# RWKV5 time mixing into a top-1 mixture of experts: order by half sequences, two padded loads a unit, w2 loads spread over the units, gate product as column tiles

## The chip, the cores and the metric

One core of a Trainium2 chip runs the whole program. Its engines work side by side and wait for each other through semaphores: TensorE (PE, with its weight loads PEld), VectorE (DVE), ScalarE (ACT), GpSimd (POOL) and SyncE (SP). Here SP issues most loads and stores; ACT issues the w2 loads and POOL the gathers and scatters by index. The metric is the device time of one execution in microseconds (us); the lower, the better.

## The reference

Two blocks follow each other. The first is a linear recurrence with 4 batches, 8 heads, 768 tokens and head size 48; the second sends each of the 3072 tokens to one of 8 experts.

```python
for t in range(S):                       # attention block, per batch and head
    cur = einsum('bhd,bhe->bhde', u * k[t], v[t])
    y[t] = einsum('bhd,bhde->bhe', r[t], state + cur)
    state = w * state + einsum('bhd,bhe->bhde', k[t], v[t])
x = y.transpose(0, 2, 1, 3).reshape(B * S, H * D)      # 3072 x 384
logits = x @ w_gate                      # 8 experts
expert = argmax(logits); gate = softmax(logits)[expert]
for e in range(8):                       # each token through its expert
    out[expert == e] = gate * (relu(x[expert == e] @ w1[e]) @ w2[e])
```

All tensors are float32.

## The kernel before, in words

**Two halves.** `fast()` computes the time mixing, `experts()` the routing and the experts. A branch on the decay values (`wi`, L78) picks `fast()` or a slower general form; with these inputs it is `fast()`. All engines read `wi` before they branch.

**Time mixing in chunks.** The sequence is cut into 6 chunks of 128 tokens. Two heads form a pair (`hp`, 4 of them), and a unit is three chunks of a pair: 4 batches x 4 pairs x 2 halves are 32 units. Unit `2i` and unit `2i + 1` are the two halves of pair `i`.

- `u_load` (L409) loads a pair on SP's queue with six DMAs: rT and kT (48 partitions for each head), kt (tokens on partitions) and V.
- `u_scale` (L420) multiplies by decay tables: K (L429), RK (L433) and Kg (L435) on POOL, R (L431) on DVE.
- `u_scores` (L439): twelve records of score products P (L448) on PE, then the u term in one column (L454). ACT copies that column (`dv`, L458) and writes six scaled identities A (L462); DVE copies P over them under a mask (L464).
- `u_state` (L472): state products Gp (L479) and the running states St on DVE (L484, L486).
- `u_out` (L489): yp from states (L501) and from A (L505), two column tiles of 64, copied by ACT to y (L508).
- `u_gate` (L510): for one chunk of 128 tokens of a batch, four products of y with IW (identity blocks and gate weights, 104 columns) into rp. ACT copies x to xb (L516), DVE reduces the logits to lg (L517). After the sixth chunk `choose` (L105) makes softmax and choice on DVE and ACT and writes xb to HBM (L125).

**Order.** Inside `manual_schedule` (L531) each engine runs its instructions in the order of the code. A step `u` issues, in this order, a pair's loads (even u), `u_scale(u + 2)`, `u_scores(u + 1)`, `u_state(u + 1)`, `u_out(u)` and one gate product, if a finished batch has some left. Six gate products of the last batch remain behind the loop.

**Tables and other loads.** The decay chain (L379 to L400) starts inside `fast()`, after the branch: seven levels of powers on DVE, two reciprocals, four transposes on PE (w3p). POOL first clears the tiles whose unused partitions must be zero (L348). All eight w2 slices (1.5 MB each) are issued on ACT's queue ahead of the branch (L725).

**DMA lanes.** Every DMA of SP and ACT takes one of eight semaphore lanes (DMAHW0 to DMAHW7) in turn, and its issue waits until the DMA that had the lane before has landed.

**Experts.** 28 tiles of 128 tokens: a gather of xs by index (L664), a load of w1 (L662), three transposes, 24 products to the hidden layer, eight to the result, a scatter.

## Time and profile before

| | us |
|---|---|
| median of 3 runs | 541.81 (541.66 to 541.88) |
| profiled execution | 540.06 |
| its span | 538.3 |
| TensorE busy | 449.0 (83%) |
| ScalarE, VectorE, GpSimd busy | 125.5, 146.6, 158.3 |

The profile is of one execution. A busy share says little here, because the program has stages with different limits: at its start loads and tables are made, then the units of time mixing run, then the last gate products and the routing, then the experts. So a view by stage comes first, then in each stage who waits for whom, and in the stage in which TensorE is busy, the chain that ended last.

In a row of the timeline or of the groups, `out<-in` names the tiles, `x12` is the number of records merged, and what stands in brackets is the engine's idle time before it and what ended that. A float32 matmul leaves two records. SPq and ACTq are the DMA issues of those queues.

### The profile page before, as it was taken

Reading aid. Unit: us, or ns where it says so; the run is one execution under the profiler, and the core shown is the slowest. Engines: PE = TensorE matmul, PEld = TensorE weight load, DVE = VectorE, ACT = ScalarE, POOL = GpSimd, SP = SyncE. Lnnn points to the kernel's source line nnn. Section 1 sums busy time; section 2 is a strip of 40 time slices with the busy share of each in tenths; the row PEclk is TensorE's granted clock in tenths of the full one; section 3 lists DMA queues with packets and bytes.
Section 4 is the critical chain, followed back from the end, with each engine's and each line's share of the span. In section 5 each row is a group of like instructions: output and inputs, shape, how many; then the busy total and the mean of one; then the engine's idle time right before and its main releaser. Section 6 shows DMA issues by size and latency. Waiting matters only on the chain.

```text
span 538.3 us, 9970 instructions
## 1 busy us (share of the span) xinstructions
PE 449.0 (83%) x3893; PEld 377.4 (70%) x3893; DVE 146.6 (27%) x376; ACT 125.5 (23%) x373; POOL 158.3 (29%) x181
## 2 busy tenths in 40 slices
PE   0027889899899730399999999999999999999994
PEld 0016889799889620288778877887788778877882
DVE  5212875646646318001010101011110101010100
ACT  0023767556557310011001100110001100110010
POOL 6017977557384000211112111211121112211220
PEclk9999999969889855599999999999999999999999
DMA  7998665385480223634554465445544554455450
GB/s 252 367 380 211 172 177 149 113 195 166 133 221 5 89 88 141 254 136 167 207 195 158 161 209 199 161 162 185 214 159 154 183 224 151 163 172 224 161 172 16
DMA packets 21900, 94.80 MB, mean 176 GB/s; under 512 B 4128, under 2 KB 7238, under 8 KB 16980
## 3 DMA queue, kind: packets, MB, share of 16 engines
q1 hardware_dynamic: 16980, 70.83, 40.5%
q0 software_dynamic: 3712, 10.64, 6.4%
q10 hardware_dynamic: 1152, 12.58, 6.3%
q8 instruction: 35, 0.57, 0.5%
q14 instruction: 21, 0.17, 0.1%
HBM read 84.59 MB, written 10.24 MB: 176 GB/s over the span
## 4 chain that ended last, share of the span: by engine, by line
PE 70%; DMA 10%; issue 9%; DVE 6%; ACT 3%; POOL 1%; ACTq 1%; POOLq 0%; DVEq 0%; SPq 0%
PE hp L685 25%; PE yp L693 23%; DMA w_all<-in_moe_w_dram 7%; PE rp L514 5%; PE P L448 4%; PE yp L505 4%; PE P L454 3%; PE yp L501 3%; PE Gp L479 2%; ACT A L462 2%; PE xTp L672 2%; DMA xs<-x_hbm,idx 1%; DVE St L486 1%; DMA x_hbm<-xb 1%; DVE A L464 1%
## 5 line engine op out<-in xcount | busy, mean ns | idle before, releaser
L685 PEld LDWEIGHTS hp<-xT,w1s 128*128 128x128 f32 x1344 | 155.8, 194 | 8.2 <-DVE xT L674 1.1
L685 PE MATMUL hp<-xT,w1s 128*128 128x128 f32 x1344 | 156.1, 277 | 0.6 <-DVE xT L674 0.6
L693 PE MATMUL yp<-w_all,hT 128*128 x448 | 149.1, 486 | 0.0
L693 PEld LDWEIGHTS yp<-w_all,hT 128*128 128x128 f32 x448 | 83.0, 190 | 51.8
L687 ACT ACTIVATE hT<-hp 128x512 f32<-128x512 f32 x56 | 33.4, 597 | 296.8 <-PE hp L685 296.8
L697 POOL DMA_INDIRECT out_dram<-yo,idx x28 | 28.5, 1019 | 248.9 <-DVE yo L696 248.9
L462 ACT ACTIVATE A<-ident,dv 128x128 f32<-128x128 f32 x192 | 59.6, 389 | 0.1
L674 DVE COPY xT<-xTp 128x384 f32<-128x384 f32 x29 | 16.2, 558 | 152.9 <-PE xTp L672 152.9
L429 POOL TENSOR_TENSOR K<-kT,W 128x384 f32<-128x384 f32 x32 | 36.2, 1132 | 57.3 <-DMA kT<-in_k_dram 31.7
L696 DVE TENSOR_SCALAR yo<-yp,xs 128x384 f32<-128x384 f32 x28 | 17.3, 618 | 129.0 <-PE yp L693 129.0
L448 PE MATMUL P<-R,K 48*128 48x128 f32 x384 | 32.7, 307 | 19.2 <-POOL K L429 15.2
L464 DVE COPY_PREDICATED A<-mask,P 128x384 f32<-128x384 int32 x64 | 33.9, 583 | 50.0 <-ACT A L462 42.7
L664 POOL DMA_INDIRECT xs<-x_hbm,idx x30 | 29.4, 981 | 56.0 <-DVE idx L650 47.2
L448 PEld LDWEIGHTS P<-R,K 48*128 48x128 f32 x384 | 26.3, 204 | 24.1 <-POOL K L429 15.7
L505 PE MATMUL yp<-A,V 128*64 128x128 f32 x384 | 42.1, 297 | 1.2 <-DVE A L464 1.1
L501 PE MATMUL yp<-R,St 128*64 128x128 f32 x320 | 35.0, 299 | 0.0
L433 POOL TENSOR_TENSOR RK<-rT,kT 128x384 f32<-128x384 f32 x32 | 34.5, 1078 | 0.0
L514 PE MATMUL rp<-IW,y 128*128 128x104 f32 x192 | 31.1, 312 | 4.0 <-DVE lg L517 4.0
L514 PEld LDWEIGHTS rp<-IW,y 128*128 128x128 f32 x192 | 26.7, 215 | 8.6 <-DVE lg L517 5.1
L505 PEld LDWEIGHTS yp<-A,V 128*64 128x64 f32 x384 | 26.9, 152 | 1.6 <-DVE A L464 1.6
L431 DVE TENSOR_TENSOR R<-rT,W 128x384 f32<-128x384 f32 x32 | 23.5, 737 | 14.6 <-DMA rT<-in_r_dram 10.3
L454 PEld LDWEIGHTS P<-wu,RK 48*128 48x128 f32 x384 | 26.8, 206 | 0.2 <-POOL RK L433 0.2
(109 smaller groups left out, 241.8 us busy)
## 6 DMA issues: line engine op xcount, KB each, us to landing
w1s<-in_moe_w_dram SPq DMA_DIRECT2D x30, 1536.0 KB, 6.8
w_all<-in_moe_w_dram ACTq DMA_DIRECT2D x8, 1536.0 KB, 20.1
x_hbm<-xb SPq DMA_DIRECT2D x4, 1155.0 KB, 5.6
rT<-in_r_dram SPq DMA_DIRECT2D x32, 144.0 KB, 3.8
kT<-in_k_dram SPq DMA_DIRECT2D x32, 144.0 KB, 3.8
kt<-in_k_tokens_dram SPq DMA_DIRECT2D x16, 288.0 KB, 4.5
V<-in_v_dram SPq DMA_DIRECT2D x16, 288.0 KB, 4.0
xs<-x_hbm,idx POOLq DMA_INDIRECT x30, 3.1
```

Source lines behind the costliest of these rows:

```text
L429: nc.gpsimd.tensor_tensor(x["K"], m["kT"][:, tt].rearrange("p (c t) -> p c t", t=C), bc(W2[:, hp, None, :], [128, HC, C]), op=ALU.mult)
L433: nc.gpsimd.tensor_tensor(x["RK"], m["rT"][:, tt], m["kT"][:, tt], op=ALU.mult)
L448: nc.tensor.matmul(P[hi][:, c * C:(c + 1) * C], lhsT=x["K"][q, c, :], rhs=x["R"][q, c, :], start=True, stop=True, skip_group_check=True)
L454: nc.tensor.matmul(P[hi][:, o:o + 1], lhsT=x["RK"][q, c * C:(c + 1) * C], rhs=wu[q, 1, hp:hp + 1], start=True, stop=True, skip_group_check ...
L462: nc.scalar.activation(A[:, hi, c, :], ident, func=ACT.Copy, scale=dv[:, hi, c:c + 1])
L464: nc.vector.copy_predicated(A[:, hi], bc(mask[:, None, :].bitcast(I32), [128, HC, C]), P[hi][:, 0:HC * C].rearrange("p (c t) -> p c t", c=HC))
L501: nc.tensor.matmul(yp[q, c, :], lhsT=m["St"][:, g, hi, :], rhs=x["R"][:, c, :], start=True, stop=False, skip_group_check=True)
L505: nc.tensor.matmul(yp[q, c, :], lhsT=vh(x, c, hi, 64), rhs=x["A"][:, hi, c, :], start=g == 0, stop=True, skip_group_check=True)
L514: nc.tensor.matmul(rp[:, hp, :], lhsT=pairs[b * HP + hp]["y"][:, ch * C:(ch + 1) * C], rhs=IW[:, hp, :], start=True, stop=True, skip_group ...
L685: nc.tensor.matmul(p[:, f, :], lhsT=m["w1"][:, d, o:o + 128], rhs=m["xT"][:, d, :], start=d == 0, stop=d == DT - 1)
L687: nc.scalar.activation(m["hT"][:, 4 * fb:4 * fb + 4, :], p, func=ACT.Relu)
L693: nc.tensor.matmul(p, lhsT=m["hT"][:, f, :], rhs=w2_all[:, ds(m["e"], 1), f * DM:(f + 1) * DM], start=f == 0, stop=f == FT - 1)
```

## The change

- **Order.** Units go by half sequences: for each batch the first halves of the four pairs, then the second halves. A unit takes its incoming state from the unit four back.
- **Loads.** The host packs r and k of a unit into one array, padded with zeros to 128 partitions, and v and k by tokens into another. A unit is two DMAs of 384 and 288 KB; before, half a pair was two of 144 KB and one of 288 KB. Rings of four and five buffers for them, and the buffers for R, K, RK and Kg, lie in the space of w2's last three slices. The first four units are issued ahead of the branch; `u_load(u + 4)` is issued at step u.
- **w2.** Slices 0 to 4 are issued on ACT's queue at steps 1, 5, 9, 13 and 17, slices 5 to 7 behind the loop.
- **Tables.** w and u come as one load on ACT's queue; the powers are made ahead of the branch. The tables for pair 0 are made first, two copies go to ACT, and one reciprocal is left. No tiles are cleared on POOL but IW and a mask.
- **Scores.** The u products stand ahead of the score products, RK ahead of K, one dv copy instead of two. There are three A tiles instead of four.
- **Gate.** A gate product is eight column tiles of 64 tokens. A half's three chunks are multiplied in the first three steps of the next half, so three are left behind the loop; these use the buffers of rp and yp. There is one xb tile instead of two.

On SP's queue, ahead of and behind the branch: `rT`, `kT`, `kt`, `V` are a pair's loads, IW the gate weights; in brackets what an issue waits for. Before:

```order
L727 TENSOR_LOAD wi [waits DVE_49]
L729 COMPARE_AND_BRANCH
L414 DMA rT_135<-in_r_dram 48x768 [waits DMAHW7_49,Pool_49]
L415 DMA kT_131<-in_k_dram 48x768 [waits DMAHW0_49]
L414 DMA rT_135<-in_r_dram 48x768 [waits DMAHW1_49]
L415 DMA kT_131<-in_k_dram 48x768 [waits DMAHW2_49]
L365 DMA IW<-in_moe_w_gate_heads_dram 48x4x8 [waits DMAHW3_49,Pool_49]
L365 DMA IW<-in_moe_w_gate_heads_dram 48x4x8 [waits DMAHW4_49]
L417 DMA kt<-in_k_tokens_dram 128x576 [waits DMAHW5_49]
L418 DMA V_147<-in_v_dram 128x576 [waits DMAHW6_49]
L414 DMA rT_136<-in_r_dram 48x768 [waits DMAHW7_49]
```

Now (`in_r_k_units` and `in_v_k_units` are a unit's two loads, written to the ring in w2's tile):

```order
L85 DMA w_all<-in_v_k_units_dram 128x576
L84 DMA w_all<-in_r_k_units_dram 128x768 [waits DMAHW0_49]
L85 DMA w_all<-in_v_k_units_dram 128x576 [waits DMAHW1_49]
L84 DMA w_all<-in_r_k_units_dram 128x768 [waits DMAHW2_49]
L85 DMA w_all<-in_v_k_units_dram 128x576 [waits DMAHW3_49]
L739 TENSOR_LOAD wi [waits DVE_49]
L741 COMPARE_AND_BRANCH
L512 DMA IW<-in_moe_w_gate_heads_dram 48x4x8 [waits DMAHW4_49,Pool_49]
L512 DMA IW<-in_moe_w_gate_heads_dram 48x4x8 [waits DMAHW5_49]
L84 DMA w_all<-in_r_k_units_dram 128x768 [waits DMAHW6_49,DVE_49]
L85 DMA w_all<-in_v_k_units_dram 128x576 [waits DMAHW7_49]
```

Four units' loads stand ahead of TENSOR_LOAD and the branch, where there was none, and the load of unit 4 stands behind IW.

On PE's queue, from the end of one unit's products to the next unit's, with a gate product between: `yp` is the unit's output, `rp` the gate product, `P` the scores. Before:

```order
L501 MATMUL yp<-R,St 64x128 x2
L505 MATMUL yp<-A_141,V_149 64x128 x2
L514 MATMUL rp<-IW,y 128x104 x4
L448 MATMUL P_943<-R,K 128x128
L448 MATMUL P_944<-R,K 128x128
```

Now (the ring's tiles read `w_all`):

```order
L495 MATMUL yp<-w_all,St 64x128 x2
L499 MATMUL yp<-A_157,w_all 64x128 x2
L527 MATMUL rp<-IW,y 64x104 x8
L447 MATMUL P<-wu,w_all 128x1 x6
L452 MATMUL P<-w_all 128x128 x6
L475 MATMUL Gp<-w_all 48x48 x6
L495 MATMUL yp<-w_all,St 64x128 x2
```

The gate product went from four products of 128 columns to eight of 64, and the u products (128x1) went ahead of the scores.

On ACT's queue, the end of the time mixing: `y` and `xb` are its copies of the unit's output and of the gate product, `ex` the choice's exponential, `hT` the experts' first step. Before, from the last unit on:

```order
L458 COPY dv<-P_2186 128x3
L458 COPY dv<-P_2187 128x3
L462 ACTIVATE A_142<-ident,dv 128x128 x6
L508 COPY y<-yp 128x384 x2
L516 COPY xb<-rp 128x384 x6
L112 ACTIVATE ex<-sub 128x48
L687 ACTIVATE hT<-hp 128x512 x56
```

Now, behind the loop:

```order
L502 COPY y<-yp 128x384
L529 COPY xb<-rp 128x384
L502 COPY y<-yp 128x384
L563 DMA w_all<-in_moe_w_dram 128x3072 x3
L529 COPY xb<-rp 128x384 x3
L150 ACTIVATE ex<-sub 128x48
L701 ACTIVATE hT<-hp 128x512 x56
```

Six gate copies behind the last unit became three, and three w2 loads stand between the last unit's copy and them.

The core of the diff:

```diff
+    wu = consts.tile([128, 2, HP], FP32, name="wu")
+    nc.scalar.dma_start(wu, wu_in)
+
+
+    ring = w2_all[:, E - 3:, :].rearrange("p e f -> p (e f)")
+    at = [0]
+
+    def cut(n, size):
+        ts = [ring[:, at[0] + i * size:at[0] + (i + 1) * size] for i in range(n)]
+        at[0] += n * size
+        return ts
+
+    rks = cut(4, 2 * HC * C)
+    toks = cut(5, 4 * HC * D)
+    Rs, Ks, RKs, Kgs = cut(3, HC * C), cut(2, HC * C), cut(2, HC * C), cut(2, 2 * HC * D)
+
+    def unit(u):
+
+        return u // (2 * HP), u // HP % 2, u % HP
+
+    def u_load(u):
+        b, hf, hp = unit(u)
+        nc.sync.dma_start(rks[u % 4], rk[b, hf, hp])
+        nc.sync.dma_start(toks[u % 5], tok[b, hf, hp])
+
+    for i in range(4):
+        u_load(i)
...
+    Wp = consts.tile([128, HP, C], FP32, name="Wp")
+    Wr = consts.tile([128, HP, C], FP32, name="Wr")
+    pw = consts.tile([128, LV + 1, HP], FP32, name="pw")
+    nc.gpsimd.memset(Wp[:, :, 0:1], 1.0)
+    nc.gpsimd.memset(Wr[:, :, C - 1:C], 1.0)
+    nc.vector.tensor_copy(pw[:, 0, :], wu[:, 0, :])
+    for l in range(LV):
+        n = 1 << l
+        wn = bc(pw[:, l, :, None], [128, HP, n])
+        nc.vector.tensor_tensor(Wp[:, :, n:2 * n], Wp[:, :, 0:n], wn, op=ALU.mult)
+        nc.vector.tensor_tensor(Wr[:, :, C - 2 * n:C - n], Wr[:, :, C - n:C], wn, op=ALU.mult)
+        nc.vector.tensor_tensor(pw[:, l + 1, :], pw[:, l, :], pw[:, l, :], op=ALU.mult)
+    wC = pw[:, LV, :]
...
+        As = [ca.tile([128, 2, HC, C], FP32, name=f"A{i}") for i in range(3)]
+
+        Gp = ps.tile([128, HC, 2, 64], FP32, name="Gp", tag="g", bufs=1)
+        nc.vector.memset(Gp, 0.0)
...
+        inv = ca.tile([128, HP, 64], FP32, name="inv")
+
+        def tables(h0, h1):
+            hs = slice(h0, h1)
+            n = h1 - h0
+            nc.vector.reciprocal(inv[:, hs], Wp[:, hs, 1:65])
+            nc.scalar.copy(W2[:, hs, 0:64], Wr[:, hs, 64:])
+            nc.scalar.copy(W2[:, hs, 64:], inv[:, hs])
+            nc.vector.tensor_tensor(W1[:, hs, 0:64], Wp[:, hs, 0:64], bc(inv[:, hs, 63:64], [128, n, 64]),
+                                    op=ALU.mult)
+            nc.scalar.copy(W1[:, hs, 64:], Wp[:, hs, 0:64])
+
+        def tables_g(h0, h1):
+            hs = slice(h0, h1)
+            n = h1 - h0
+            W3 = As[2].rearrange("p h c t -> p (h c t)")[:, 0:HP * C].rearrange("p (a t) -> p a t", a=HP)
+            nc.vector.tensor_tensor(W3[:, hs], Wr[:, hs], bc(pw[:, LV - 1, hs, None], [128, n, C]), op=ALU.mult)
+            w3p = ps.tile([128, HP, C], FP32, name="w3p", tag="rw", bufs=1)
+            for hp in range(h0, h1):
+                nc.tensor.transpose(w3p[:, hp, :], W3[:, hp, :], ident)
+            nc.scalar.copy(Wg[:, hs], w3p[:, hs].rearrange("p a (h d) -> p a h d", h=2)[:, :, :, 0:D])
...
-            nc.gpsimd.tensor_tensor(x["K"], m["kT"][:, tt].rearrange("p (c t) -> p c t", t=C),
-                                    bc(W2[:, hp, None, :], [128, HC, C]), op=ALU.mult)
-            nc.vector.tensor_tensor(x["R"], m["rT"][:, tt].rearrange("p (c t) -> p c t", t=C),
-                                    bc(W1[:, hp, None, :], [128, HC, C]), op=ALU.mult)
-            nc.gpsimd.tensor_tensor(x["RK"], m["rT"][:, tt], m["kT"][:, tt], op=ALU.mult)
+            nc.gpsimd.tensor_tensor(x["RK"], x["r"], x["k"], op=ALU.mult)
+            nc.gpsimd.tensor_tensor(x["K"], x["k"], bc(W2[:, hp, None, :], [128, HC, C]), op=ALU.mult)
+            nc.vector.tensor_tensor(x["R"], x["r"], bc(W1[:, hp, None, :], [128, HC, C]), op=ALU.mult)
...
-            P = x["P"] = [ps.tile([128, 512], FP32, name=f"P{hi}", tag=f"P{hi}", bufs=2) for hi in range(2)]
-            for c in range(HC):
-                for hi in range(2):
-                    q = slice(64 * hi, 64 * hi + D)
-                    nc.tensor.matmul(P[hi][:, c * C:(c + 1) * C], lhsT=x["K"][q, c, :], rhs=x["R"][q, c, :],
-                                     start=True, stop=True, skip_group_check=True)
+            hp, A = x["hp"], x["A"]
+            P = ps.tile([128, 2, 512], FP32, name="P", tag="P", bufs=2)
             for c in range(HC):
                 for hi in range(2):
                     q = slice(64 * hi, 64 * hi + D)
                     o = HC * C + c
-                    nc.tensor.matmul(P[hi][:, o:o + 1], lhsT=x["RK"][q, c * C:(c + 1) * C],
+                    nc.tensor.matmul(P[:, hi, o:o + 1], lhsT=x["RK"][q, c, :],
                                      rhs=wu[q, 1, hp:hp + 1], start=True, stop=True, skip_group_check=True)
+            for c in range(HC):
+                for hi in range(2):
+                    q = slice(64 * hi, 64 * hi + D)
+                    nc.tensor.matmul(P[:, hi, c * C:(c + 1) * C], lhsT=x["K"][q, c, :], rhs=x["R"][q, c, :],
+                                     start=True, stop=True, skip_group_check=True)
             dv = ap2.tile([128, 2, HC], FP32, name="dv")
-            for hi in range(2):
-                nc.scalar.copy(dv[:, hi, :], P[hi][:, HC * C:HC * C + HC])
-            A = x["A"] = As[u % NA]
+            nc.scalar.copy(dv, P[:, :, HC * C:HC * C + HC])
...
+            x["y"] = ca.tile([128, HC * C], FP32, name="y", tag="y", bufs=8)
+            nc.scalar.copy(x["y"], yp.rearrange("p c t -> p (c t)"))
...
+                gx[b] = (ca.tile([128, G, W], FP32, name="xb"), sm.tile([128, G, E], FP32, name="lg"))
+            xb, lg = gx[b]
+            ch = hf * HC + c
+            rp = ps.tile([128, HP, 2 * D + E], FP32, name="rp", tag=tag, bufs=bufs)
             for hp in range(HP):
-                nc.tensor.matmul(rp[:, hp, :], lhsT=pairs[b * HP + hp]["y"][:, ch * C:(ch + 1) * C],
-                                 rhs=IW[:, hp, :], start=True, stop=True, skip_group_check=True)
+                y = units[h * HP + hp]["y"]
+                for j in range(2):
+                    q = slice(64 * j, 64 * j + 64)
+                    nc.tensor.matmul(rp[q, hp, :], lhsT=y[:, c * C + 64 * j:c * C + 64 * j + 64],
+                                     rhs=IW[:, hp, :], start=True, stop=True, skip_group_check=True)
...
-
-        gates = []
+            if ch == G - 1:
+                choose(b, xb, lg)
+
         gx = {}
 
-        def gate_step():
-            b, ch = gates.pop(0)
-            if ch == 0:
-                gx[b] = (ap2.tile([128, G, W], FP32, name="xb"), sm.tile([128, G, E], FP32, name="lg"))
-            u_gate(b, ch, *gx[b])
-            if ch == G - 1:
-                choose(b, *gx[b])
-
         with tc.manual_schedule():
-            u_load(0)
-            u_load(1)
+            tables(0, 1)
             u_scale(0)
+            tables_g(0, HP)
+            u_scale_g(0)
+            tables(1, HP)
+            u_scores(0)
             u_scale(1)
-            u_scores(0)
+            u_scale_g(1)
+            gate_weights()
             u_state(0)
             for u in range(NU):
-                if u % 2 == 0 and u // 2 + 2 < B * HP:
-                    u_load(u // 2 + 2)
+                if u + 4 < NU:
+                    u_load(u + 4)
+                if u % 4 == 1 and u // 4 < E - 3:
+                    nc.scalar.dma_start(w2_all[:, u // 4, :], w2[u // 4])
                 if u + 2 < NU:
                     u_scale(u + 2)
+                    u_scale_g(u + 2)
                 if u + 1 < NU:
                     u_scores(u + 1)
                     u_state(u + 1)
                 u_out(u)
-                if gates:
-                    gate_step()
-                if u % (2 * HP) == 2 * HP - 1:
-                    gates += [(u // (2 * HP), ch) for ch in range(G)]
-            while gates:
-                gate_step()
+                if u >= HP and u % HP < HC:
+                    u_gate(u // HP - 1, u % HP, "rw", 1)
+            for e in range(E - 3, E):
+                nc.scalar.dma_start(w2_all[:, e, :], w2[e])
+            u_gate(NU // HP - 1, 0, "rw", 1)
+            u_gate(NU // HP - 1, 1, "y", 2)
+            u_gate(NU // HP - 1, 2, "y", 2)
...
-    for e in range(E):
-        nc.scalar.dma_start(w2_all[:, e, :], w2[e])
```

## Rows read from the trace of the kernel before

**Rows 1.** Stages: start:end, length; busy PE, PEld, DVE, ACT, POOL; clock, DMA share, GB/s.

```profile
0.00:44.64 44.64, 4.46 (x40) 3.95 (x40) 13.19 (x45) 3.37 (x9) 13.90 (x33) 1.00 0.89 317
44.64:180.20 135.56, 126.14 (x1903) 116.77 (x1901) 84.41 (x214) 85.15 (x300) 86.47 (x91) 0.94 0.59 155
180.20:201.65 21.45, 10.70 (x51) 8.97 (x50) 2.62 (x15) 3.59 (x8) 0.00 (x0) 0.59 0.19 69
...
224.00:538.30 314.30, 306.32 (x1879) 246.32 (x1879) 33.49 (x57) 33.43 (x56) 54.91 (x55) 0.99 0.48 168
```

**Rows 2.** Waits of SP's queue, 0 to 45 us: total, times, longest.

```profile
SPq L415 <- DMA w_all<-in_moe_w_dram: 11.4, 2, 6.6
...
SPq L365 <- DMA w_all<-in_moe_w_dram: 8.0, 2, 4.4
```

**Rows 3.** Timeline, first 53 us: start, length, engine, line, tiles; idle before and releaser.

```profile
2.94 0.54 DVE L73 TENSOR_REDUCE wx<-wrow 1x1 f32<-1x384 f32 x1 [1.57 <-DMA wrow<-in_w_row_dram]
...
7.97 0.54 DVE L379 COPY pw<-wu 128x4 f32<-128x4 f32 x1 [2.64 <-DMA wu<-in_w_dram]
...
14.42 1.69 DVE L392 RECIPROCAL W<-Wp 128x256 f32<-128x256 f32 x1
...
16.80 1.09 PE L398 MATMUL w3p<-ident,W 128*128 128x128 f32 x4 [16.80 <-DVE W L395]
...
31.40 0.99 POOL L429 TENSOR_TENSOR K<-kT,W 128x384 f32<-128x384 f32 x1 [18.78 <-DMA kT<-in_k_dram]
...
44.64 1.65 PE L448 MATMUL P<-R,K 48*128 48x128 f32 x12
...
47.30 0.56 PE L479 MATMUL Gp<-V,Kg 128*48 128x48 f32 x8
```

**Rows 4.** DMA listing, all: queue, count, KB each, median us to landing.

```profile
x_hbm<-xb SPq DMA_DIRECT2D x4, 1155.0 KB, 5.6
...
wu<-in_w_dram SPq DMA_DIRECT2D x2, 0.8 KB, 6.0
```

**Rows 5.** Line L726 (the w2 loads on ACT's queue): ns of an issue, min/median/max.

```profile
L726 ACTq DMA_DIRECT2D w_all<-in_moe_w_dram x8: 334/448/797, 0.8 to 10.6; - x8
```

**Rows 6.** Timeline of PE: first score matmuls of four time-mixing steps.

```profile
57.44 0.94 PE L448 MATMUL P<-R,K 48*128 48x128 f32 x12
...
64.34 0.94 PE L448 MATMUL P<-R,K 48*128 48x128 f32 x12
...
79.22 0.94 PE L448 MATMUL P<-R,K 48*128 48x128 f32 x12
...
95.53 0.94 PE L448 MATMUL P<-R,K 48*128 48x128 f32 x12
```

**Rows 7.** Chain that ended last, 83 to 88 us: one step with a gate product.

```profile
83.52 0.87 PE P L448 x12
84.39 0.56 PE P L454 x11
84.95 0.32 PE Gp L479 x8
...
85.50 0.22 PE yp L501 x4
...
86.37 1.07 PE rp L514 x8
```

**Rows 8.** Timeline: two waits after a routing choice.

```profile
104.90 0.96 PE L448 MATMUL P<-R,K 48*128 48x128 f32 x12 [2.22 <-DVE R L431]
...
150.32 1.02 POOL L429 TENSOR_TENSOR K<-kT,W 128x384 f32<-128x384 f32 x1 [9.44 <-DMA kT<-in_k_dram]
```

**Rows 9.** Timeline of the tail: gate product, last routing choice, first routing step.

```profile
184.00 1.89 PE L514 MATMUL rp<-IW,y 128*128 128x104 f32 x8 [0.80 <-DVE lg L517]
...
195.15 0.20 DVE L108 TENSOR_REDUCE mx<-lg 128x6 f32<-128x48 f32 x1
...
201.65 0.36 DVE L573 COPY rk<-rkp 128x192 f32<-128x192 f32 x1 [4.55 <-DMA x_hbm<-xb]
```

201 lines of the change are left out of this document (77 added, 124 removed).

## The prediction

> **What bounds the kernel now.** I first read busy time by stage [rows 1]. There are four stages: 44.64 us before the second score product, 135.56 us of time mixing, 21.45 us of tail, and, after 22.35 us of routing and first gather, 314.30 us of experts. TensorE is busy for 306 of the last stage's 314 us, and the change does not touch that code. It is busy for 4.46 us of the first stage and 10.70 us of the tail, so these two hold most of the idle time.
>
> Second, who waits in the first stage. The four loads of a pair stand on SP's queue. Of its time, 11.4 us before the kT issues and 8.0 us before the IW issues go to w2 transfers [rows 2]: a load's issue waits for a semaphore lane (DMAHW) that a w2 load took before it, so the loads go out one by one as the w2 slices land. GpSimd has its first K at 31.40 us, after 18.78 us of idle time that ends with the kT load; the steady loop begins at 44.64 us [rows 3].
>
> Third, the loop. A step without a gate takes 3.45 us, (64.34 - 57.44) / 2; one with a gate takes 4.08 us, (95.53 - 79.22) / 4 [rows 6]. In the gated step the chain is TensorE alone: 0.87 + 0.56 + 0.32 + five products at 0.22 + 1.07 = 3.92 us [rows 7]; with six products and a state product of 3 chunks it is 4.2. Without the gate that leaves 3.0 us, so the ungated step waits some 0.45 us for others. All 32 steps at these rates: 9.0 for the first two (44.64 to 53.63, slow clock), 18 x 4.08, 11 x 3.45 and 1.4 for the last step, 121.8 us. The loop took 135.6. The 13.8 us of difference lie at the three routing choices inside it: VectorE's choice delays R, and TensorE waits 2.22 us; the xb write stands on SP's queue ahead of the next loads, and a K waits 9.44 us for kT [rows 8]; the clock then falls (0.94 over the stage [rows 1]).
>
> Fourth, the tail. Six gate products stand one behind another, since each needs the one rp buffer back: 1.89 us of product after 0.80 us of waiting [rows 9]. The first routing step waits 4.55 us for the xb write.
>
> **Start: -28.2 us.** Loads of four units are issued before the branch and no w2 load is ahead of them, so the decay chain is next. Before, it runs from 7.97 (pw) to 17.89 (the end of w3p), 9.9 us [rows 3]. To this are added two reductions at 0.54, and the branch, which I put at 0.6; the two full reciprocals (1.7 each) shrink to a quarter of one, 0.4, ahead of W3, and two copies go to ACT: about 8.9 us. It starts when wu has landed. That is at about 3.0 us if it lands like wrow (2.94 [rows 3]), 3.5 us later if it takes the 6.0 us of the old wu loads [rows 4]. So w3p ends near 12. Unit 0's scores take 2.66 us (44.64 to 47.30) and its state product 0.6, and P of unit 1 starts near 15.5 by TensorE. GpSimd's queue holds RK, K, Kg of unit 0 and RK, K of unit 1 in a row at 1 us each, which allows 15 to 16.5. I take 16.4 for the point that was 44.64. The bounds are 14.5 and 20: -30 to -24.6. The first steps at slow clock are kept as they are.
>
> **Loop: -6.6 us.** Three gate products come into it (21 instead of 18).
> The gate product becomes eight column tiles of 64. The nearest row is u_out's pair of column tiles at 0.22 us for 128 columns [rows 7]; with 104 columns, four pairs cost 0.72 to 0.88, and 1.07 is the upper bound. I take 0.85, so a gated step is 3.85.
> As to the Trainium skill, TensorEngine Tiling (Array Packing), section Restrictions and Gotchas: column tiling and the fast weight load exclude each other. By that rule, with nothing gained, a gate would stay at 1.07 and the loop be 4.6 us longer; the 0.22 us pair, which loads its 64-column weights within that time, speaks for the smaller value.
> RK's product moves ahead of the scores, so ACT's A chain starts 0.87 us sooner; one dv copy is saved. An ungated step falls from 3.45 towards TensorE's 3.0: 3.2. Then 9.0 + 21 x 3.85 + 8 x 3.2 + 1.4 = 116.9 us. The order by half sequences leaves the number of state instructions as it is.
> The choices remain on VectorE's queue ahead of the next R, and the RK product now in front of P covers 0.6 of the 2.22 us. A load is issued four units ahead, so the 9.44 us wait should go. But two things are added. The x tile has one buffer, not two: the first gate copy of a batch waits on ACT for the xb write of the batch before (5.6 us to landing [rows 4]), and behind it stand dv and six A copies, for which VectorE and then TensorE wait. And five w2 loads now run beside the units' loads, at 0.45 us of ACT each to issue [rows 5], which ACT's idle time (85 busy of 136 us [rows 1]) hides. I take 4 us for each of three choices, 12 in all: 129 us against 135.6. The bounds are 0 and the old 13.8 with no gain at gates or ungated steps (+6.8) and 3 us for xb: 117 to 141.
> The loads themselves: a unit moves 0.69 MB, padding included; 22.0 MB of units, 7.9 of w2 and 3.5 of xb make 33.4 MB in the loop. The old loop moved 155 GB/s at a DMA share of 0.59, so 263 GB/s would fill the engines [rows 1]: 127 us of transfers. That is close to the loop's length, and closer still while w2 runs (rival 2).
>
> **Tail: -14.7 us.** Three gates remain, on three buffers (rw and the two of y). Products 2.6 us, beside them ACT: y copy 0.5, three w2 issues at 0.45 [rows 5], three xb copies at 0.5, then the last reduction 0.2, about 3.9 us after the last u_out; choice and two rank products took 1.95 (195.15 to 201.65 - 4.55 [rows 9]). The wait of 4.55 us for xb goes, because the routing tile no longer waits for a DMA. Some 6.8 us with handovers, against 21.45: bounds 5.5 and 9.5. In its place comes nothing on VectorE; the xb write is next, and only the gather needs it, some 15 us later.
>
> **Routing and experts: 0.** The same instructions; the last three w2 slices land during routing. Bounds -1 and +3.
>
> **Sum.** 540.06 us of the profiled execution (span 538.3) - 28.2 - 6.6 - 14.7 = 490.6. The median of the runs is 1.75 us above that execution, so I give **492.3 us**. By the bounds of the terms, 476 to 514.
>
> **Rivals.**
> 1. The choices stay as dear as they are, or the xb copy's wait on ACT replaces the late load and the clock falls again: loop 141, 504 us. For it: a stall of 2 us was enough before [rows 8]. Against: four units of loads ahead.
> 2. The transfers bound the first half. Eighteen steps, 69 us, have 12.4 MB of units, 7.9 of w2 and 1.2 of xb: 21.5 MB, 82 us at 263 GB/s, so +13 less the 4 that a choice would have cost anyway: 501 us. Against: the start moved 317 GB/s [rows 1], at which 21.5 MB take 68 us.
> The Trainium skill, Trainium Kernel Development and Optimization, section Key Constraints, says that transfers from the SP, ACT and POOL queues share the same 16 DMA engines and interleave; by it w2 on ACT's queue takes its time from the units' loads, as rival 2 has it.
> 3. Everything hides: no stall at a choice, loop 117, 480 us. Against: VectorE's choice is as long as before.
> 4. The last w2 slices hold up the xb write and with it the gather. They are 4.7 MB, 15 us at 317 GB/s, with xb's 5.6 behind them: 21 us, about when the gather asks. If it is late, +6: 498 us.
> 5. The start does not do what it says: the branch, ACT's copies and GpSimd's queue put 44.64 at 25, not 16.4: 501 us.
> 6. Slower than before. If the small padded rows beside w2 and xb moved no faster than the old loop's mean of 155 GB/s, 33.4 MB would need 215 us against 129: 578 us. It decides below 33.4 MB / 178 us = 188 GB/s. Against: 0.59 is the share at 155, the engines were not full.
>
> **How the numbers follow.** Forecast 0.56, rivals 1 to 6: 0.13, 0.09, 0.11, 0.04, 0.05, 0.02. The forecast's own spread is about 485 to 499; the range takes in rivals 2, 4, 5 and part of 1 and 3: 481 to 503 us. Only rival 6 is slower: slower by over 0.2% (about what a measurement of this kernel can tell from no change) 0.02, within 0.2% 0.01, faster 0.97.
>
> **What would show it.** Start: the second unit's first score product near 16 us and SP's queue without waits for w_all. Loop: gated steps near 3.85 us, rp groups near 0.85; at each choice look for ACT's xb copy waiting for x_hbm<-xb and for K waiting for a unit's load. Tail: some 7 us from the last yp to rk, whose wait is for PE, not a DMA. Wrong would be: a DMA share near 1 through the first half, K waiting for loads in most steps, or a gather later than the index by more than 8 us.

## The result and the profile after

Median of the runs 493.63 us (492.04 to 494.36), before 541.73 us; the ratio is 0.911 with an interval of 0.909 to 0.914. The forecast was 492.3 us. The profiled execution took 493.97 us with a span of 492.2 us, against 540.06 and 538.3 us before: 46.1 us less, where the terms summed to 49.5. The median hides part of that gap, because the profiled execution of before was 1.67 us under its median and this one is 0.3 us above its own. So the 1.3 us by which the median missed is not the size of the errors; those stand in the stages.

The stages of the kernel after, cut at the points that answer to [rows 1] (second score product, first gate product of the tail, first routing copy, first expert product; columns: start:end, length, busy time of PE, PEld, DVE, ACT and POOL, granted clock, DMA share, GB/s):

```profile
0.00:19.14 19.14, 5.97 (x52) 5.30 (x53) 11.70 (x39) 5.18 (x15) 11.05 (x30) 1.00 0.42 145
19.14:147.66 128.52, 119.18 (x2081) 109.75 (x2082) 86.00 (x217) 84.76 (x272) 84.07 (x89) 0.97 0.69 241
147.66:153.43 5.77, 2.87 (x54) 2.24 (x50) 2.05 (x11) 2.01 (x5) 0.00 (x0) 1.00 0.75 268
153.43:178.22 24.79, 2.30 (x28) 1.85 (x28) 13.37 (x46) 0.00 (x0) 3.08 (x3) 0.51 0.91 351
178.22:492.20 313.98, 306.95 (x1876) 247.25 (x1876) 32.93 (x56) 33.44 (x56) 55.00 (x55) 0.98 0.49 172
```

| stage | before, us | after, us | moved | forecast |
|---|---|---|---|---|
| start, to the second score product | 44.64 | 19.14 | -25.5 | -28.2 |
| loop, to the first product of the tail | 135.56 | 128.52 | -7.0 | -6.6 |
| tail, to the first routing copy (rk) | 21.45 | 5.77 | -15.7 | -14.7 |
| routing and first gather, to the first expert product | 23.92 | 24.79 | +0.9 | 0 |
| experts | 312.73 | 313.98 | +1.25 | 0 |

(The first expert product of before begins 1.55 us behind the 224.02 at which the stage of [rows 1] was cut, at 225.57 us, so the last two lines are cut there.)

**Start.** The timeline of the kernel after (start, length, engine, line, tiles; in brackets the idle time before and what ended it):

```profile
2.56 0.17 DVE L107 COPY pw<-wu 128x4 f32<-128x4 f32 x1 [2.56 <-DMA wu<-in_w_u_dram]
...
13.50 1.63 PE L452 MATMUL P<-w_all 48*128 48x128 f32 x12
...
17.09 1.05 DVE L460 COPY_PREDICATED A<-mask,P 128x384 f32<-128x384 int32 x2 [4.40 <-ACT A L458]
...
18.03 0.96 DVE L428 TENSOR_TENSOR w_all<-w_all,W 128x384 f32<-128x384 f32 x1
...
19.14 1.66 PE L452 MATMUL P<-w_all 48*128 48x128 f32 x12 [1.99 <-DVE w_all L428]
```

Against [rows 3] the decay chain starts at 2.56 instead of 7.97 us, and w3p ends at 12.27 (forecast: near 12). The waits of SP's queue for w2 in [rows 2] have no successor: no wait of that queue before 45 us names a w2 load. What is new is the last wait: the second score product stands for 1.99 us until VectorE has made R of unit 1, and VectorE had been standing in front of unit 0's predicated copies, which wait for ScalarE's A tiles.

**A choice.** In the same view, step 11, where before there was [rows 8]:

```profile
65.06 0.85 DVE L157 SCALAR_TENSOR_TENSOR eq<-sub,rev_e 128x48 f32<-128x48 f32 x1
...
67.18 0.94 PE L452 MATMUL P<-w_all 48*128 48x128 f32 x12 [1.57 <-DVE w_all L428]
...
67.89 0.72 DVE L482 SCALAR_TENSOR_TENSOR St<-St,pw,Gp 128x128 f32<-128x128 f32 x2
...
68.71 0.56 PE L475 MATMUL Gp<-w_all 128*48 128x48 f32 x8 [0.59 <-issue]
...
70.34 0.67 PE L499 MATMUL yp<-A,w_all 128*64 128x128 f32 x4
...
...
72.67 0.48 ACT L529 COPY xb<-rp 128x384 f32<-128x384 f32 x1 [0.29 <-PE rp L527]
```

R still stands behind the choice, and TensorE still waits (1.57 us, before 2.22). The state product behind it waits another 0.59 us: it writes the one Gp bank that VectorE's state (to 68.61 us) reads, and it starts 0.10 us behind that. Then four output products take 0.67 us where they otherwise take 0.39: the granted clock is 0.50 from 68.7 to 71 us, the lower of its two levels (1.2 and not 2.4 GHz). The two steps behind the first and behind the third choice took

```profile
62.50:73.23 10.73, 8.57 (x128) 7.92 (x128) 7.65 (x22) 5.51 (x18) 3.17 (x4) 0.84 0.69 216
...
130.18:138.74 8.56, 7.09 (x129) 6.45 (x128) 6.91 (x21) 5.03 (x17) 2.51 (x3) 1.00 0.59 188
```

With the second choice's 10.22 that is 29.51 us, where three undisturbed pairs (3.27 + 3.89) would be 21.48: 8.0 us for the choices. (A pair that holds a choice without any wait takes 7.6 us, as experiment 9 will show; against that it is 6.7.) ScalarE's x copy, whose wait for the xb write was part of rival 1, starts behind TensorE and waits for no transfer. GpSimd's RK waits 6.1 us there, but four units are loaded ahead, and no product waits for it.

**Tail and routing.** Three gate products in a row (2.60 us for 48 matmuls, where one of [rows 9] took 1.89), the rank copy without a transfer in front of it, then a gather that is not sooner and a first expert product at a low clock:

```profile
147.66 2.60 PE L527 MATMUL rp<-IW,y 128*64 128x104 f32 x48
...
153.43 0.36 DVE L587 COPY rk<-rkp 128x192 f32<-128x192 f32 x1 [0.43 <-PE rkp L583]
...
166.28 2.12 SPq L676 DMA_DIRECT2D w1s<-in_moe_w_dram  x3
...
169.06 1.18 POOL L678 DMA_INDIRECT xs<-x_hbm,idx  x1 [26.47 <-DVE idx L664]
...
176.61 0.90 PE L686 MATMUL xTp<-ident,xs 128*128 128x128 f32 x3 [9.33 <-DMA xs<-x_hbm,idx]
...
178.22 8.58 PE L699 MATMUL hp<-xT,w1s 128*128 128x128 f32 x48 [0.71 <-DVE xT L688]
```

The w1s loads are asked for 12.9 us behind rk, because SP waits there for the xb write (5.0 us, the only wait of that queue for a DMA before them in this stage), and the xb write shares the engines with three w2 slices: the stage has a DMA share of 0.91. The gather is issued 15.6 us behind rk, as before, but lands 7.5 us after its issue, where before it took 6.7. The first 48 expert products took 7.04 us before; the granted clock was 0.50 up to 228 us then, 2.4 us from the first of them, and is 0.50 up to 184 us now, 5.8 us from it.

### The profile page after: what moved, and what is told of

The parts are those of the page before. It is cut to its first block, busy times and chain, and to the rows that moved or that the text cites. A ratio compares the mean times of both kernels' runs of the same rounds, so it can differ in the third digit from the quotient of the medians.

```text
span 492.2 us, 10185 instructions
## 1 busy us (share of the span) xinstructions
PE 437.3 (89%) x4085; PEld 366.4 (74%) x4085; DVE 146.0 (30%) x368; ACT 125.4 (25%) x348; POOL 153.2 (31%) x176
## 5 line engine op out<-in xcount | busy, mean ns | idle before, releaser
L711 POOL DMA_INDIRECT out_dram<-yo,idx x28 | 28.6, 1020 | 251.1 <-DVE yo L710 242.6
L426 POOL TENSOR_TENSOR w_all<-w_all 128x384 f32<-128x384 f32 x32 | 34.6, 1081 | 39.3 <-PE P L452 8.3
L499 PE MATMUL yp<-A,w_all 128*64 128x128 f32 x384 | 41.4, 288 | 0.0
L427 POOL TENSOR_TENSOR w_all<-w_all,W 128x384 f32<-128x384 f32 x32 | 35.8, 1120 | 2.8 <-ACT W L393 2.8
L452 PE MATMUL P<-w_all 48*128 48x128 f32 x384 | 30.9, 295 | 5.3 <-DVE w_all L428 5.3
L495 PE MATMUL yp<-w_all,St 128*64 128x128 f32 x320 | 34.1, 288 | 0.0
L452 PEld LDWEIGHTS P<-w_all 48*128 48x128 f32 x384 | 25.4, 197 | 5.5 <-POOL w_all L426 2.0
L447 PEld LDWEIGHTS P<-wu,w_all 48*128 48x128 f32 x384 | 25.3, 197 | 4.9 <-issue 1.3
L447 PE MATMUL P<-wu,w_all 48*128 48x1 f32 x384 | 28.1, 258 | 0.0
L499 PEld LDWEIGHTS yp<-A,w_all 128*64 128x64 f32 x384 | 26.4, 145 | 0.4 <-DVE A L460 0.4
L428 DVE TENSOR_TENSOR w_all<-w_all,W 128x384 f32<-128x384 f32 x32 | 26.1, 816 | 0.2 <-ACT W L396 0.2
```

What stands on the lines that cost most here:

```text
L426: nc.gpsimd.tensor_tensor(x["RK"], x["r"], x["k"], op=ALU.mult)
L427: nc.gpsimd.tensor_tensor(x["K"], x["k"], bc(W2[:, hp, None, :], [128, HC, C]), op=ALU.mult)
L447: nc.tensor.matmul(P[:, hi, o:o + 1], lhsT=x["RK"][q, c, :], rhs=wu[q, 1, hp:hp + 1], start=True, stop=True, skip_group_check=True)
L452: nc.tensor.matmul(P[:, hi, c * C:(c + 1) * C], lhsT=x["K"][q, c, :], rhs=x["R"][q, c, :], start=True, stop=True, skip_group_check=True)
L495: nc.tensor.matmul(yp[q, c, :], lhsT=old[:, hi, :], rhs=x["R"][:, c, :], start=True, stop=False, skip_group_check=True)
L499: nc.tensor.matmul(yp[q, c, :], lhsT=vh(x, c, hi, 64), rhs=x["A"][:, hi, c, :], start=old is None, stop=True, skip_group_check=True)
```

## Experiments

All of them are the kernel after with an edit. Medians taken on different chips differ by 1 to 3 us, so the verdicts rest on stages of the profiled executions; the medians stand beside them. In the text a step is the time from one unit's score product to the next one's.

**1. The gate product as 4 products of 128 columns.**

```diff
-                for j in range(2):
-                    q = slice(64 * j, 64 * j + 64)
-                    nc.tensor.matmul(rp[q, hp, :], lhsT=y[:, c * C + 64 * j:c * C + 64 * j + 64],
+                nc.tensor.matmul(rp[:, hp, :], lhsT=y[:, c * C:(c + 1) * C],
```

> The gate product is one matmul of 128 columns per head pair again (4 instead of 8 column tiles of 64). Theory of the prediction (column tiles are cheaper): a gate goes from 0.71 to 0.82 us between its start and that of the next product to 1.07 us as before the change, so 24 gates cost 24 x 0.3 = some 7 us: about 500 us, the gated step near 4.2 instead of 3.9 us. Rival (other engines set the gated step, or the column tiles gain nothing because their weight loads are slow): the gated step stays at 3.9 us and the time within 1 us of 493.6.

Measured: 496.86 us median, ratio to before 0.918 (0.910 to 0.926). PE's timeline, one gated step of this kernel, and then of the kernel after:

```profile
72.70 0.92 PE L452 MATMUL P<-w_all 48*128 48x128 f32 x12
...
75.19 1.14 PE L525 MATMUL rp<-IW,y 128*128 128x104 f32 x8
...
76.95 0.92 PE L452 MATMUL P<-w_all 48*128 48x128 f32 x12
```

```profile
73.23 0.92 PE L452 MATMUL P<-w_all 48*128 48x128 f32 x12
...
75.62 0.88 PE L527 MATMUL rp<-IW,y 128*64 128x104 f32 x16
...
77.12 0.92 PE L452 MATMUL P<-w_all 48*128 48x128 f32 x12
```

4.25 against 3.89 us: the column tiles are worth some 0.35 us a gated step (0.30 in the mean of the 17 gated steps outside the choices). Yet the loop was only 2.0 us longer, and not 5 to 7: its three choices took 8.90 us each, 26.7 in all against 29.51, at a granted clock of 1.00 throughout, though its products waited 0.85 to 0.89 us there.

```profile
63.80:72.70 8.90, 7.46 (x120) 6.68 (x120) 6.90 (x21) 5.03 (x17) 2.50 (x3) 1.00 0.64 179
```

So the theory of the step holds, and the faster step loses part of its gain at the choices, where its clock falls. Why the clock held in this kernel behind waits of the same length is not shown.

**2. Scores ahead of the RK products.** The two loops of L447 and L452 change places.

> The score products stand ahead of the RK products again. Theory of the prediction (RK first lets ScalarE start the A tiles 0.87 us sooner): the dv copy moves 0.87 us later in the step, the step without a gate goes from 3.27 to about 3.5 us. Rival (the dv columns lie in the same PSUM bank as the scores, so the copy waits for the last product of the bank in either order): the dv copy follows the last of the 24 products as before, the step without a gate stays at 3.27 us, and only where R is late does TensorE wait longer: about 0.8 us at each of three choices and 1.4 us at the start, since the RK products no longer cover it. Theory: 493.6 + 8 x 0.25 + 4 = about 499.5 us; rival: about 497.5 us, with all of it at those four places.

Measured: 497.72 us median, 0.920 (0.914 to 0.925), near the rival's figure, though not by its terms. Ungated steps took 3.16 us and most gated ones 3.79, even 0.1 us less than with RK first; the loss is at the choices (10.8 us for the two steps, three times, clock 0.84: 3.0 us more in all). The start lost only 0.2 us by unit 6's score product (39.33 us, against 39.11), where the rival had 1.4. The profiled execution is 2.8 us longer than that of the kernel after. Where ScalarE's dv copy starts, first in the kernel after, then in this one:

```profile
142.63 0.92 PE L452 MATMUL P<-w_all 48*128 48x128 f32 x12
...
143.59 0.17 ACT L455 COPY dv<-P 128x6 f32<-128x6 f32 x1 [1.03 <-PE P L452]
```

```profile
84.65 0.73 PE L452 MATMUL P<-wu,w_all 48*128 48x1 f32 x12
...
85.45 0.16 ACT L455 COPY dv<-P 128x6 f32<-128x6 f32 x1 [0.74 <-PE P L452]
```

In either order the copy starts 0.04 to 0.07 us behind the last product of both groups, though it reads columns that only the RK products write. "ACT's A chain starts 0.87 us sooner" did not happen. The Trainium skill, PSUM — Partial Sum Buffer, section PSUM bank collisions raise a hardware error, says why it cannot: two engines may not touch the same bank and 32-partition quadrant at once, other columns included, and the compiler puts a dependency between them. The trace agrees, by these 0.04 to 0.07 us.

**3. Five w2 slices at the very start.** The spread is undone; the eight early unit loads stay.

> The five w2 slices that the change spreads over the loop are issued at the very start on ScalarE's queue; the eight unit loads stay as they are on SP's. Theory (a queued load that waits for a semaphore lane holds its whole engine, as before the change): ScalarE's table copies stand behind w2 issues that wait for lanes, SP's loads of units 2 and 3 wait too, and the second score product goes from 19.1 to some 30 us: about 503 to 506 us. Rival (only the engines of the DMA are shared, and the first units' 1.4 MB interleave with w2): the start is 2 to 4 us longer, the loop up to 2 us shorter because it has 7.9 MB fewer to move: 493 to 496 us.

Measured: 504.66 us median, 0.934 (0.926 to 0.942), within the theory's figures. The timeline of its start:

```profile
1.23 13.95 ACTq L67 DMA_DIRECT2D w_all<-in_moe_w_dram  x5
...
18.62 1.28 ACT L394 ACT_TABLE_LOAD   x1 [18.62 <-DMA x_hbm<-zrow]
...
30.51 1.65 PE L454 MATMUL P<-w_all 48*128 48x128 f32 x12 [1.99 <-DVE w_all L430]
```

ScalarE is held by its own w2 issues until 18.6 us, and the table copies, R and K stand behind it. The second score product moves by 11.4 us, the span by 9.7, and the loop (128.25 us) is hardly shorter for the 7.9 MB that it no longer moves. It is the issues that cost at the start, and in the loop the w2 transfers cost nothing that this run shows.

**4. R of unit 1 ahead of unit 0's A tiles.** `u_scale(1)` moves one line up, ahead of `u_scores(0)`.

> Unit 1's scaled R, K and RK are asked for ahead of unit 0's A tiles, so that VectorE makes R of unit 1 before it waits for ScalarE's A tiles. Theory (the forecast missed the start by 2.7 us because R of unit 1 stands behind the two predicated copies, which wait for the A tiles): the 2.0 us wait of the second score product goes, it starts near 17.2 instead of 19.1 us, and the time is 491.6 us. Rival (K of unit 1 or the RK products would be late anyway, or the first steps wait for GpSimd): the start gains under 0.5 us, the time stays at 493 to 494 us.

Measured: 492.64 us median, 0.911 (0.905 to 0.918); span 490.6. The wait went and the second score product moved to 16.99 us, as the theory has it. But of these 2.1 us nothing is left at the score product of unit 6, which starts at 39.11 us in both kernels:

```profile
16.99 1.63 PE L452 MATMUL P<-w_all 48*128 48x128 f32 x12
...
39.11 0.92 PE L452 MATMUL P<-w_all 48*128 48x128 f32 x12
```

Two things took its place: the state product of unit 1 now waits 0.54 us for VectorE's state of unit 0 (the state ends at 19.06, the product starts at 19.16 us), and the products run slow for longer: the first score products that take 0.92 us come at 28.22 us, in the kernel after at 24.44. The 0.6 us by which the loop ends sooner come at the first choice, where the wait is 0.87 instead of 1.57 us.

**5. Unread products first.**

```diff
+            idle = ps.tile([128, C], FP32, name="idle", tag="rw", bufs=1)
+            for i in range(22):
+                nc.tensor.matmul(idle, lhsT=ident, rhs=ident, ...)
             tables(0, 1)
```

> 22 products of the identity with itself, which nobody reads, stand on TensorE's queue ahead of the table transposes. Theory (the first products run at half their later rate, 1.66 against 0.92 us for twelve, because TensorE idled before): the first steps run at the later rate, the second score product starts 1 to 1.5 us sooner and the steps up to 24.4 us gain 2 us: about 490.5 us. Rival (the first rate has another cause, or the chain at the start is VectorE's and ScalarE's alone): within 1 us of 493.6.

Measured: 490.39 us median, 0.909 (0.900 to 0.917); span 489.2. PE's timeline:

```profile
13.53 0.92 PE L452 MATMUL P<-w_all 48*128 48x128 f32 x12
...
18.04 1.65 PE L452 MATMUL P<-w_all 48*128 48x128 f32 x12 [1.90 <-DVE w_all L428]
```

Unit 0's scores take 0.92 instead of 1.63 us: what TensorE did before sets the rate. Behind the 1.90 us wait for R it is back at 1.65. The second score product came 1.1 us sooner, in the theory's range; the 2 us in the first steps did not come, as the products were slow again from that wait on: unit 6's score product starts at 38.11 us, 1.0 us sooner. The loop ends 1.6 us sooner, and the rest of the 3 us lies in the experts, which the edit does not touch, so the median near the theory's 490.5 is in part luck. Experiment 9 has the edits of 4 and 5 together.

**6. The choice cut in three.** mx, sub, eq, m2 and the one-hot row move behind R and ahead of the predicated copies, the exponential behind the A tiles, the rest behind the state; two xb tiles.

> The routing choices inside the loop are cut up: the five steps that need no exponential stand behind R on VectorE's queue and ahead of the predicated copies, the exponential behind the A tiles, the last three steps behind the state; the x tile has two buffers. Theory (a choice ahead of R makes TensorE wait 0.9 to 1.6 us, and the slow clock after it costs more): the two steps after a choice, which took 10.73, 10.22 and 8.56 us, fall to some 7.2 us each, 8 us in all: about 485.5 us. Rival (the late unit loads behind the xb write on SP's queue, GpSimd's wait of 6 to 7 us there, are what costs): the two steps stay at 8.5 us or more and the time above 490 us.

Measured: 496.06 us median, 0.915 (0.907 to 0.924): no gain. The two steps took 10.6, 10.4 and 10.7 us, so by its numbers the theory fell. The timeline shows how (L486 are the predicated copies, L508 the state, L501 the state product):

```profile
67.58 0.71 DVE L508 SCALAR_TENSOR_TENSOR St<-St,pw,Gp 128x128 f32<-128x128 f32 x2
...
68.39 0.56 PE L501 MATMUL Gp<-w_all 128*48 128x48 f32 x8 [2.11 <-POOL w_all L453]
```

R's wait is gone (the first of the two steps fell from 4.68 to 2.96 us), but the predicated copies and the state now stand behind the choice, and the next state product needs the one Gp bank that the state reads: it waits 2.11 us (the profile names GpSimd, whose K had ended at 67.60; the state ended at 68.29). The clock falls at all three choices (0.84 over the two steps). The rival's late loads are not it either: no product waits for one. The revised theory is one of amount: of a step of 3.27 us VectorE needs 0.55 for R, 1.05 for the predicated copies and 0.72 for the state, so it has under 1 us to spare, and a choice takes 2.5 to 3.2 us there from its first to its last operation, wherever it stands.

**7. One w2 slice earlier, two behind the choice.**

> Of the last three w2 slices one is asked for in the last but one step of the loop, as soon as the unit loads that used its place are read, and the other two behind the last routing choice. Theory (the xb write shares the DMA engines with 4.7 MB of w2, the first w1s load waits for its landing until 166.3 us, and the gather then runs beside all three w1s loads): the xb write lands some 4 us sooner, w1s is asked for near 162 us, the first expert product starts 3 to 4 us sooner: 489.5 to 490.5 us. Rival (the gather's 7.5 us is its own latency or is set by w1s alone): within 1 us of 493.6.

Measured: 492.99 us median, 0.911 (0.907 to 0.916). From the first rank product to the first expert product it is 25.5 us, in the kernel after 25.2: no gain in the routing. SP's wait for the xb write is 5.9 us, in the kernel after 5.0. This decides nothing, since the edit did not do what it was for: the two slices went out at 149.85 us, still ahead of the xb write at 150.69, and w1s was asked for at 165.14 us, 13.5 us behind rk. Experiments 9 to 12 do put two slices behind that write.

**8. Unread products in the routing.**

> 44 such products stand on TensorE's queue between the index products of the routing and the first transpose of the experts (16 of them ahead of the index products). Theory (the granted clock of 0.50 in the routing is what makes the first 48 expert products take 8.58 instead of 5.52 us): they take 5.6 to 6 us and the time falls by 3 us to about 490.5 us. Rival (the first products wait for w1s): no gain, 493 to 494 us, or up to 1 us more where the added products end after the gather.

Measured: 494.75 us median, 0.915 (0.911 to 0.920): no gain. PE's timeline:

```profile
178.18 0.90 PE L686 MATMUL xTp<-ident,xs 128*128 128x128 f32 x3 [3.08 <-DMA xs<-x_hbm,idx]
...
179.79 7.73 PE L699 MATMUL hp<-xT,w1s 128*128 128x128 f32 x48 [0.70 <-DVE xT L688]
```

The 16 in front delayed the index products by 2.8 us and the issue of the gather by 2.2; the 28 behind ran out 3.08 us too soon, and the expert products took 7.73 us (8.58 in the kernel after). This one was inconclusive on the theory; experiment 12 decides it.

**9 to 12. Together.** Nine holds a version for each stage: 17 unread products at the start, the gate weights and RK of unit 1 earlier on GpSimd's queue, R and K of unit 1 early; each choice in four parts at the ends of four steps; the reduction ahead of the x copy in the tail; the last two w2 slices on SP behind the xb write; 49 unread products behind the index products.

```diff
+                now = pend.pop(0) if pend else None
                 if u >= HP and u % HP < HC:
                     u_gate(u // HP - 1, u % HP, "rw", 1)
+                if now:
+                    now()
```

> Several changes, each in a stage of its own. Start: 17 unread products on TensorE first, the gate weights and RK of unit 1 earlier on GpSimd's queue, R and K of unit 1 ahead of unit 0's A tiles. Loop: each choice in four parts, two VectorE operations at the end of each of four steps, two x tiles. Tail: the reduction for the choice ahead of the x copy. Routing: the last two w2 slices on SP's queue behind the xb write, one slice two steps earlier, 49 unread products behind the index products. Theory: a choice is some 2 to 3 us of VectorE in a step that has 0.8 us to spare, so cutting it into 0.4 us parts frees R and the state product alike, the clock does not fall, and the two steps after a choice take 7.2 us instead of 8.6 to 10.7: loop -7 us; second score product near 14.7 instead of 19.1 us, first steps at the later rate: -5 us; routing -3 us: about 478 us. Rival (as in the last trial of the choices, the wait turns up at another product and the clock falls all the same): the two steps stay at 10 us, 485 us.

> The same, with the score products ahead of the RK products. Theory (the shorter step seen with that order, 3.78 and 3.16 instead of 3.89 and 3.27 us, holds once no choice stands ahead of R): 28 x 0.11 = 3 us less than the kernel of the same call that has RK first: about 475 us. Rival (R is late in other steps too, and RK first covers it): no gain or 1 to 3 us more.

> The same as the one with the scores first, with the state product behind the output products of the step. Theory (the state product waits for Kg on GpSimd, 0.7 us at three steps and 0.2 to 0.6 us at six more): some 3 us less, about 472 us. Rival (the state then comes late for the next output products, or VectorE's queue is only put in another order): no gain.

> The last combined kernel (scores first, state product behind the output products) with three numbers changed: 27 instead of 49 unread products in the routing, 19 instead of 17 at the start, and the five w2 slices of the loop asked for in the prologue and at steps 5, 10, 18 and 25 instead of at 1, 5, 9, 13 and 17. Theory: the 49 products ran to 172 us, 4 to 5 us beyond the time at which the transfers of the gather were through, so the first expert product starts some 28.6 - 4 = 24.6 us behind the rank product instead of 29.1 us, at the same rate (48 products in 5.6 us); and the steps that took 4.5 to 5.2 us for late unit loads fall to 3.7 to 3.8 us, 2 us: 476 to 478 us. Rival (TensorE's clock falls again in the gap between the added products and the gather, and the late loads do not depend on w2): first expert products 7.5 to 8.5 us, steps unchanged: 480 us or more.

| kernel | median, us | ratio to before | second score product | loop | rank product to first expert product |
|---|---|---|---|---|---|
| after | 493.63 | 0.911 (0.909 to 0.914) | 19.1 | 128.5 | 25.2 |
| 9: all stages | 486.93 | 0.898 (0.888 to 0.908) | 15.8 | 124.5 | 28.6 |
| 10: + scores first | 485.13 | 0.893 (0.885 to 0.901) | 15.8 | 121.7 | 29.4 |
| 11: + state product behind the outputs | 482.53 | 0.886 (0.878 to 0.895) | 16.0 | 123.1 | 29.1 |
| 12: + three numbers | 481.44 | 0.887 (0.881 to 0.894) | 15.8 | 122.3 | 25.1 |

The choices, in nine: the revised theory holds. All three pairs of steps took 7.6 us (7.2 expected) at a clock of 1.00:

```profile
61.90:69.50 7.60, 6.95 (x130) 6.37 (x128) 6.42 (x15) 5.52 (x18) 5.33 (x6) 1.00 0.63 197
```

Scores first, in ten: steps of 3.79 and 3.16 instead of 3.89 and 3.27 us, as the theory has them, and the loop is 2.8 us shorter. But 2.4 us of that lie ahead of unit 6's score product, where ten's products come to the later rate sooner (at 24.64 us, in nine at 27.57); behind it the shorter steps leave 0.4 us, as one K comes late and its product waits 0.97 us. State product last, in eleven: the step that was 4.54 us is 3.68, and a wait of 0.81 us of the state product is gone. The profile names Kg (L472) for that wait, as the theory did, but Kg had ended at 78.84 us; VectorE's state of the unit before (L521) ended at 79.54, and the product started 0.10 us behind it. It is the one Gp bank of experiment 6, and the new order gives VectorE the time of the output products. First the step in ten, then in eleven:

```profile
77.33 0.94 PE L485 MATMUL P<-w_all 48*128 48x128 f32 x12
...
79.64 0.47 PE L514 MATMUL Gp<-w_all 128*48 128x48 f32 x12 [0.81 <-POOL w_all L472]
...
81.87 0.94 PE L485 MATMUL P<-w_all 48*128 48x128 f32 x12
```

```profile
79.28 0.94 PE L485 MATMUL P<-w_all 48*128 48x128 f32 x12
...
82.96 0.94 PE L485 MATMUL P<-w_all 48*128 48x128 f32 x12
```

Its loop as a whole was no shorter than ten's, since the first steps ran at the slow rate until 32 us (22 us in ten; why is open) and two steps waited for late loads; its profiled execution (486.44 us) is also the longest of its four. The start in all four: 15.8 to 16.0 us where 14.7 was expected, and not at the later rate for long. In nine, which has the edits of 4 and 5 together, unit 6's score product starts at 38.46 us, no sooner than with 22 unread products alone (38.11): the state product of unit 1 waits 1.64 us for VectorE's state of unit 0, which stands behind the predicated copies, and the products are slow again behind it. So it is that chain that bounds the first steps, once R is out of the way. The routing of nine to eleven got worse, as 49 unread products ran to 4 us or so past the gather's transfers; with 27 of them, in twelve, it shows what experiment 8 could not:

```profile
158.21 8.11 PE L784 MATMUL idle<-ident 128*128 128x128 f32 x52
...
166.71 0.55 PE L746 MATMUL xTp<-ident,xs 128*128 128x128 f32 x3 [0.39 <-DMA xs<-x_hbm,idx]
...
167.96 5.62 PE L759 MATMUL hp<-xT,w1s 128*128 128x128 f32 x48 [0.70 <-DVE xT L748]
```

5.62 us for the first 48 expert products instead of 8.58. (In twelve w1s was asked for sooner too, but in the kernel after these products stand without a wait between them, so it is the clock.) The gather itself is no sooner: its transpose starts 23.8 us behind the first rank product, in the kernel after 23.6, though SP asks for w1s 7.6 us behind that product there, and in the kernel after 13.2 us. Holding back the w1s loads of the second and third tile, which share the engines with it, was not tried.

The other numbers of twelve missed: late loads did not go, they moved. Two K come 1.6 us late for lack of their loads (VectorE's R of the same units names the load; the DMA share is 1.02 at 78 to 84 and at 112 to 118 us), and the clock falls over the second:

```profile
121.59 1.65 PE L485 MATMUL P<-w_all 48*128 48x128 f32 x12 [1.61 <-POOL w_all L462]
```

```profile
121.00:129.00 8.00, 7.41 (x78) 7.26 (x80) 5.10 (x10) 2.77 (x10) 6.37 (x8) 0.57 0.06 23
```

Eleven and twelve cannot be told apart by their medians; both are some 12 us below the kernel after.

## Why the prediction was right, and where not

In the profiled execution the gain was 3.4 us short of the sum: start 2.7, routing and experts 2.1, against 1.0 more in the tail and 0.4 in the loop.

**Start (-28.2; measured -25.5, inside its bounds).** wu, the decay chain, w3p and unit 0 came as worked out. The step that failed is "P of unit 1 starts near 15.5 by TensorE", with GpSimd's queue as the only other limit: VectorE's queue was left out. R of unit 1 stands there behind unit 0's predicated copies and so behind ScalarE's A chain; experiment 4 shows it. But that wait by itself is not what the 2.7 us cost: with it gone, unit 6 came no sooner, since the next link of the chain, VectorE's state of unit 0, held TensorE instead. That "no w2 load is ahead of them" gives 11.4 us of it, experiment 3 shows: with the early loads kept and w2 in front again, these are lost. The larger part, the unit loads' order on SP against w2, was not undone by itself.

**Loop (-6.6; measured -7.0), by errors that cancel.** The gate at 0.85: its group took 0.88 us, the next product came 0.81 to 0.85 us behind its start (with the four wide products 1.06 to 1.07), and experiment 1 puts the step at 0.35 us less. The Trainium skill's rule that column tiling and fast weight load exclude each other (TensorEngine Tiling (Array Packing), Restrictions and Gotchas) would have left nothing; the measurement decides for the gain. Another page of the Trainium skill (TensorE: Matmul & The Clock Gate, Weight-path perf modes) says that fast weight load is off for FP32 inputs; these are FP32, so by that there was nothing to lose, and the rule should not have been weighed here. The gated step, put at 3.85, was 3.76 to 3.90 where nothing waited, but 4.05 on average over the 17 outside the choices: 3.4 us more than forecast. Some 3.3 us of that are waits of the state product in seven of them:

```profile
51.79 0.47 PE L475 MATMUL Gp<-w_all 128*48 128x48 f32 x12 [0.71 <-POOL w_all L426]
```

The profile names GpSimd's RK, which this product does not read. VectorE's state of the unit before, which reads the one Gp bank, ended at 51.69 us. All eleven such waits of the loop end 0.10 us behind that state, whatever the profile names. The choices were put at 12 us and cost 8.0.

What was wrong in kind is the reason given for the ungated step (3.2; measured 3.27). The dv copy did not start sooner (experiment 2), and RK first in fact makes the step 0.1 us longer; it pays where R is late. Nor did TensorE in before wait 0.45 us in each ungated step. The 3.45 us were a mean of two: a step without any wait (57.44 to 60.60 us, [rows 6], 3.16 us) and one of 3.74 us, in which the state product waits for the state:

```profile
60.60 0.94 PE L448 MATMUL P<-R,K 48*128 48x128 f32 x12
...
62.92 0.39 PE L479 MATMUL Gp<-V,Kg 128*48 128x48 f32 x8 [0.81 <-DVE St L486]
```

In the kernel after, the ungated steps between gated ones (3.27 us) have no such wait; from unit 5 on it stands in gated steps and behind the choices. The prediction put the order of units at nothing here; which part of the change moved the wait, no run shows by itself.

**Tail (-14.7; measured -15.7).** Right in each part: three products 2.60 us, no wait for the xb write. The 1.0 us more is what the sum kept for handovers: 3.9 and 1.95 are 5.85 us, and it took 5.77. No run undoes this part by itself.

**Routing and experts (0; measured +2.1).** "The same instructions" at 0 was the step that failed, by two terms. The gather took 0.8 us longer from issue to landing, beside the w1s loads, at a DMA share of 1.01 from 169 to 176.6 us. And the first 48 expert products took 8.58 instead of 7.04 us, as the granted clock stayed at 0.50 for 5.8 us of them; twelve shows the clock's part, but why it came back later than before is open. "The last three w2 slices land during routing" holds, and SP's first w1s load waits behind them for the xb write; that this costs anything is not shown, for in twelve w1s was asked for over 5 us sooner and the gather came no sooner. It is rival 4's place and a third of its price, but not its mechanism: the gather was issued as early behind rk as before.

**Rivals.** Rival 1 was half there: the choices stayed VectorE's and the clock fell at two of three, but the x copy never waited for the xb write (at the first, the write's 6.6 us had just ended). Rival 2 did not show in this kernel: the loop moved 241 GB/s at a share of 0.69 (287 at 0.81 in its first half, where the w2 slices are), and experiment 3 took 7.9 MB out of it without a gain. It is the next bound all the same: in twelve, with the loop at 122 us, loads come late. Rival 6 asked for 188 GB/s or less.
